# Seven products per expert in a written order over four PSUM rings, the f16 part of h three products later, the squares of the next W1 in the second product

## The chip, the cores and the metric

The kernel runs on one core of a Trainium2 chip. The metric is the device time of one execution in microseconds, as the median of the runs; the run shown by the profile is one execution of its own. Engines are named as in the profile: PE is the matmul engine, PEld its weight loads, DVE the vector engine, ACT the scalar engine, POOL GpSimd, SP the engine whose queue issues the DMAs.

## The reference

Three layers follow each other. Attention over q, k, v (2 x 8 heads x 576 x 64) gives x, 1152 tokens by 512. A mixture of eight experts follows, in which every expert sees every token:

```
P = exp(x @ w_gate - max); 8 times: rows to sum 1, columns to sum N / 8
out = sum over e of P[:, e] * (relu(x @ w1[e]) @ w2[e])      # w1[e]: 512 x 1024, w2[e]: 1024 x 512
```

A last feed-forward layer uses h = out @ w_in, g = h * tanh(softplus(h)), g @ w_out, with w_in and w_out in float64. Inputs and result of the experts are float32.

## The kernel before

**Arithmetic.** A float32 operand is scaled by a power of two and cut into an f16 part (`hi`) and an f16 rest (`lo`); a product is hi·hi + hi·lo + lo·hi, three matmuls per piece of 128 rows. The scale of a weight matrix comes from its sum of squares: four ACT operations (L234, each with an accumulator read behind it), a DVE sum, a POOL all-reduce and some small DVE operations (L64 to L74).

**First product of an expert** (`G1_7`, experts 1 to 7; expert 0 runs another way). x @ w1[e] is done by Winograd's form of Strassen with seven half-size products M1 to M7 instead of eight. There are eight groups (2 token halves of 576 x 4 columns of 128), so 56 products of six matmuls (L966, 288 columns each) in one stage. In a group M1, M6, M5 and M3 accumulate one after the other in one PSUM bank; between them ACT copies the running sum out (L935, a snap: s1, s2, s3). M2 has a bank of its own, M7 and M4 share a third. DVE adds a snap to M2, M7 and M4 (L939), ACT copies M3 out (L980); two halves make a row `r` of 576 tokens. `parts` then lets ACT write the f16 part of relu(r) to h (L947) and DVE, three products later, the rest (L948). A product that accumulates in a bank must wait until the snap of its predecessor has been read.

**Order.** `order7` places the 56 products by due times and by distances (four products from M1 to M6, M6 to M5, M5 to M3). Where nothing fits it leaves a gap, in which `fill` does one of the eight pieces of the second product's first tile (`Head`). Every group takes its three banks from all eight in turn (`mm_tile`).

**Second product** (`G2`): nine tiles of 128 tokens, each 24 matmuls of 512 columns (L995) into one bank, and a DVE operation (L1024) that adds the tile, times P, to acc.

**Work in the background.** Generators in three queues move by one step at each `tick`, in both products. In the first product of expert e: squares and scale of W2[e], its f16 parts (ACT L210, DVE L223), then the load of W1[e+1] and its squares and scale. In the second product: the sums of W1[e+1] that Strassen needs with their f16 parts (`sums_gen`, ACT L266, DVE L269, L273), then the load of W2[e+1]. W1 and W2 share two raw buffers. A third queue (`spare`) converts w_in and w_out from float64 (`Split64`, DVE L343 to L359, L381, L384, L409; ACT L331, L380, L383, L403) over experts 1 to 6. Each engine runs its instructions in the order in which the program issues them, and so does SP with its DMAs.

Of the kernel before, what the change touches and what calls it, by code (L numbers as in the profile page):

```python
# [21 lines left out]
def attn_moe_moe2_kernel(ctx: ExitStack, tc: tile.TileContext, q, k, v, w_gate, w1, w2, w_in, w_out, out):  # L22
# [203 lines left out]
    class SplitSq(Split):  # L226


        def scale_gen(self):
            mx = sm.tile([128, 4], F32, tag="sq", name="sq")  # L230
            for i, r in enumerate(self.raw):
                for c in range(2):
                    junk = late["junk"].tile([128, 1024], BF16, tag="junk", name="junk")
                    nc.scalar.activation(out=junk, in_=r[:, c * 1024:(c + 1) * 1024], func=AF.Square,  # L234
                                         accum_out=mx[:, 2 * i + c:2 * i + c + 1])
                    yield
            m1 = sm.tile([128, 1], F32, tag="m1", name="m1")
            nc.vector.tensor_reduce(out=m1, in_=mx, axis=AX.X, op=ALU.add)  # L238
            ma = all_max(m1)
            for _ in range(3):  # L240
                yield
            self.s, self.inv = scale_from_squares(ma, "sc_" + self.name, self.spare)
            yield

    class SplitSums(SplitSq):
# [56 lines left out]
    class Split64:  # L302
# [94 lines left out]
        def parts_out(self, f, a, b, m):  # L397


            sc = s_out[:, f, :]  # L400
            powers(exponent(m), 266, sc)
            for w in (a, b):
                nc.scalar.activation(out=w, in_=w, func=AF.Copy, scale=sc.bitcast(F32)[:, 0:1])  # L403
            yield
            t = self.w32()
            hw = CW // 2

            def sub(out, u, v):
# [411 lines left out]
    def mm_banks(n):  # L820
        i = len(mm_pools)
        mm_pools.extend([(ps_pool(f"mm{i}", n), f"mm{i}")] * n)
# [71 lines left out]
    SEVEN = dict(M1=(A11_, "B11", "X", None), M6=(S2_, 1, "X", "M1"), M5=(S1_, 0, "X", "M6"), M3=(S4_, "B22", "X", "M5"),  # L894
                 M2=(A12_, "B21", "Y", None), M7=(S3_, 2, "Z", None), M4=(A22_, "T4", "Z", "M7"))

    def order7():


        at = dict(M1=0, M6=4, M2=5, M5=8, M7=9, M3=13, M4=17)  # L900
        todo = sorted((7 * g + t, g, m) for g in range(FT) for m, t in at.items())
        when, order = {}, []
        while todo:
            n = len(order)
            for t, g, m in todo:
                before = SEVEN[m][3]
                if m in "M2 M7" and (g, "M1" if m == "M2" else "M5") not in when:
                    continue
                if t <= todo[0][0] + 14 and (not before or n - when.get((g, before), n) >= (6 if m == "M4" else 4)):
                    when[g, m] = n  # L910
                    order.append((g, m))
                    todo.remove((t, g, m))
                    break
            else:
                order.append(None)
        return order

    def G1_7(w, h, fill):

        open_, lows = {}, []

        def factor(b, n, p, i):
            if n == "T4":
                return xs[b][:, p, i, CH:2 * CH]
            if isinstance(n, str):
                k, j = int(n[1]) - 1, int(n[2]) - 1
                return xs[b][:, p, 2 * k + i, j * CH:(j + 1) * CH]  # L930
            return xt[b][:, p, n, i, :]
# [12 lines left out]

        def parts(n, b, f, r):
            hi, lo = [h[f][:, p, 2 * b * CH:2 * (b + 1) * CH] for p in range(2)]
            nc.scalar.activation(out=hi, in_=r, func=AF.Relu)  # L947
            lows.append((n + 3, lambda: nc.vector.scalar_tensor_tensor(out=lo, in0=r, scalar=0.0, in1=hi, op0=ALU.max,  # L948
                                                                       op1=ALU.subtract)))

        for n, item in enumerate(order7()):
            if item is None:
                fill()
            else:
                gi, m = item
                b, f = gi // 4, gi % 4
                g = open_.setdefault(gi, {})
                a, bn, bank, before = SEVEN[m]
                if not before:
                    g[bank] = mm_tile()[:, 0:CH]  # L960
                ps = g[bank]
                k = 0
                for i in range(2):
                    for wi, xi in ((0, 0), (0, 1), (1, 0)):
                        c = i * 512 + f * 128
                        nc.tensor.matmul(ps, lhsT=w.part(wi, a)[:, c:c + 128], rhs=factor(b, bn, xi, i),  # L966
                                         start=(not before and k == 0), stop=(k == 5), skip_group_check=True)
                        k += 1
                if m == "M1":
                    g["s1"] = snap("s1", ps, 2)  # L970
                elif m == "M6":
                    g["s2"] = snap("s2", ps, 3)
                elif m == "M5":
                    g["s3"] = snap("s3", ps, 2)
                elif m == "M2":
                    add(row(g, "r1")[:, 0:CH], ps, g["s1"])
                elif m == "M7":
                    add(row(g, "r2")[:, CH:2 * CH], ps, g["s3"])
                elif m == "M3":
                    nc.scalar.activation(out=g["r1"][:, CH:2 * CH], in_=ps, func=AF.Copy, scale=HSC)  # L980
                    parts(n, b, f, g["r1"])
                else:
                    add(g["r2"][:, 0:CH], ps, g["s2"])
                    parts(n, b, f + 4, g["r2"])
            while lows and lows[0][0] <= n:
                lows.pop(0)[1]()
            if n % 2 or n % 8 == 0:
                tick(more=n % 6 == 5)
        while lows:
            lows.pop(0)[1]()  # L990

    def G2_products(ps, w, h, t, ft):
        ws = slice(ft * DM, (ft + 1) * DM)
# [4 lines left out]
    class Head:  # L998
# [5 lines left out]
        def __call__(self):  # L1004
            assert self.w.whole and self.n < FT
            if self.ps is None:
                self.ps = mm_tile()
            G2_products(self.ps, self.w, self.h, 0, self.n)
            self.n += 1

    def G2(e, w, h, t, pc, between=None, head=None):
        ps = head.ps if head and head.n else mm_tile()
        for ft in range(FT):
            if not head or ft >= head.n:
                G2_products(ps, w, h, t, ft)
# [90 lines left out]
    with tc.manual_schedule():  # L1106
# [90 lines left out]
        for nm, n in (("junk", 1), ("r", 6), ("wx", 1), ("ws", 1), ("xt", 1), ("sn", 1)):  # L1197
            late[nm] = sb_pool("late_" + nm, n, late_cm)

        early_cm = ExitStack()  # L1200
# [26 lines left out]
        first.drain()  # L1227
        second.drain()
        sp_cm.close()
        mm_banks(2)  # L1230

        def finish(e):
            pc = const.tile([128, NTT], F32, name=f"pc{e}")
# [27 lines left out]
        for e in range(1, E):  # L1261
            h = new_h()
            if e == 1:
                second.add(W2[1].scale_gen(), W2[1].split_gen(), float64_gen(), scale0_gen(), W1[2].scale_gen())
            else:
                second.add(wait_gen(2), W2[e].scale_gen(), W2[e].split_gen())
                if e + 1 < E:
                    second.add(load_gen(W1[e + 1], 8), W1[e + 1].scale_gen())
            head = Head(W2[e], h)
            G1_7(W1[e], h, head)  # L1270
            second.drain()
            pc = finish(e)
            if e + 1 < E:
                second.add(W1[e + 1].sums_gen(), wait_gen(2), load_gen(W2[e + 1], 0))
                for t in range(NTT):
                    G2(e, W2[e], h, t, pc, head=None if t else head)
                second.drain()
# [319 lines left out]
```

## Time and profile before

| | |
|---|---|
| three runs | 1035.18, 1035.9, 1037.35 us; median 1035.9 |
| span of the profiled execution | 1034.6 us, so about 1.3 us of the median lie around the span |
| PE busy | 978.5 us, 95% of the span |
| DVE, ACT, POOL busy | 724.6 us (70%), 510.6 us (49%), 98.0 us (9%) |
| chain that ended last, by engine | PE 73%, DVE 12%, ACT 9%, DMA 2%, issue 2% |
| its costliest lines | L995 34%, L966 15%, L1379 9%, L1446 8%, L939 2%, L948 2%, L210 2%, L234 2% |

The profile was taken in one execution, whose own total time is not listed apart from the span. Busy shares are means over stages with different limits. From 204.56 us (first product of expert 1) to 804.53 us (rest of the second product of expert 7) the program alternates between first and second products, and nearly all of that time PE is busy. A busy PE row overlaps its neighbour: two successive matmuls start closer together than one is shown to last.

### The profile page before, as it was taken

The numbers are of one execution on the slowest core, as the hardware profiler recorded it, in microseconds if no ns is written. First come the engines' busy times: TensorE is split into PE (matmuls) and PEld (weight loads), VectorE is DVE, ScalarE is ACT, GpSimd is POOL, SyncE is SP. The second block draws the span as 40 slices with busy tenths as digits, with TensorE's granted clock in tenths as the row PEclk, the third lists the DMA queues.
The fourth block names the chain that finished last, engine by engine and source line by source line (L and its number), as shares of the span: only waits on it lengthen the run. The fifth ranks groups of instructions, "written<-read, shape, count | busy, mean of one in ns | idle before, by whom it ended". The sixth has DMA issues, their size and how long they took to land.

```text
span 1034.6 us, 17830 instructions
## 1 busy us (share of the span) xinstructions
PE 978.5 (95%) x7185; PEld 656.4 (63%) x7185; DVE 724.6 (70%) x1552; ACT 510.6 (49%) x951; POOL 98.0 (9%) x127
## 2 busy tenths in 40 slices
PE   5889998888999999999999999999999999999998
PEld 4567565466467547645754664575467566988897
DVE  7788649657968796796879669787936456545531
ACT  5667435266357727634672674276346222333431
POOL 6653244000000000000000000000000000000000
PEclk9669998999999999999999999999999999999999
DMA  8962020201243151315314221521300710100010
GB/s 166 211 170 83 17 82 1 81 31 53 84 142 123 50 173 41 123 44 182 122 41 156 70 112 51 183 77 47 133 11 1 316 50 21 68 16 16 6 63 32
DMA packets 83589, 89.25 MB, mean 86 GB/s; under 512 B 34610, under 2 KB 67890, under 8 KB 82226
## 3 DMA queue, kind: packets, MB, share of 16 engines
q1 hardware_dynamic: 83506, 88.11, 27.1%
q8 instruction: 56, 0.92, 0.4%
q14 instruction: 27, 0.22, 0.1%
HBM read 73.15 MB, written 14.94 MB: 85 GB/s over the span
## 4 chain that ended last, share of the span: by engine, by line
PE 73%; DVE 12%; ACT 9%; DMA 2%; issue 2%; POOL 1%; SPq 1%; DVEq 0%; POOLq 0%; ACTq 0%
PE mm L995 34%; PE mm L966 15%; PE mm L1379 9%; PE n L1446 8%; PE mm L845 3%; DVE r L939 2%; DVE h L948 2%; ACT wbh L210 2%; ACT junk L234 2%; ACT h L947 2%; ACT s L935 1%; DMA raw<-in_moe_w_dram 1%; DVE wbl L223 1%; PE at L587 1%; PE at L742 1%
## 5 line engine op out<-in xcount | busy, mean ns | idle before, releaser
L995 PE MATMUL mm<-wbh,h 128*128 128x512 f16 x1152 | 360.0, 382 | 0.0
L995 PEld LDWEIGHTS <-h 128*128 128x128 f16 x1728 | 168.6, 99 | 191.6 <-issue 6.6
L995 PE MATMUL mm<-wbl,h 128*128 128x512 f16 x576 | 220.1, 382 | 0.0
L966 PE MATMUL mm<-x,wah 128*128 128x288 f16 x672 | 129.2, 286 | 0.0
L939 DVE SCALAR_TENSOR_TENSOR r<-mm,s 128x288 f32<-128x288 f32 x168 | 75.2, 454 | 72.1 <-PE mm L966 39.0
L966 PEld LDWEIGHTS <-wx 128*128 128x128 f16 x1008 | 98.6, 98 | 33.8 <-issue 8.4
L966 PEld LDWEIGHTS <-wah 128*128 128x128 f16 x896 | 87.5, 98 | 48.1 <-issue 22.7
L947 ACT ACTIVATE h<-r 128x576 f16<-128x576 f32 x112 | 76.3, 683 | 74.7 <-DVE r L939 72.5
L1379 PE MATMUL mm<-xc,win 128*128 128x256 f16 (+1 forms) x960 | 107.6, 262 | 0.0
L966 PE MATMUL mm<-xt,wx 128*128 128x288 f16 x672 | 100.6, 286 | 3.2 <-ACT s L935 3.2
L966 PE MATMUL mm<-x,wal 128*128 128x288 f16 x336 | 96.1, 286 | 0.0
L1379 PEld LDWEIGHTS <-win 128*128 128x128 f16 x960 | 87.2, 98 | 13.3
L948 DVE SCALAR_TENSOR_TENSOR h<-r,h 128x576 f16<-128x576 f32 x112 | 84.0, 750 | 1.2 <-ACT h L947 1.1
L935 ACT ACTIVATE s<-mm 128x288 f32<-128x288 f32 x168 | 65.3, 399 | 39.2 <-PE mm L966 38.8
L1388 ACT ACTIVATE tt<-mm,cf 128x512 f32<-128x512 f32 (+1 forms) x40 | 25.8, 645 | 113.1 <-PE mm L1379 111.3
L1395 DVE TENSOR_TENSOR tt<-tt 128x128 f32<-128x128 f32 x128 | 31.6, 288 | 68.8 <-ACT tt L1388 67.7
L95 POOL PARTITION_ALL_REDUCE ma<-m x25 | 10.9, 438 | 651.0 <-DVE m L238 397.7
L966 PE MATMUL mm<-xt,wah 128*128 128x288 f16 x224 | 43.4, 285 | 18.6 <-ACT s L935 18.4
L1024 DVE SCALAR_TENSOR_TENSOR acc<-mm,pc,acc 128x512 f32<-128x512 f32 x63 | 46.6, 745 | 14.7 <-PE mm L995 14.5
L234 ACT ACTIVATE junk<-raw 128x1024 bf16<-128x1024 f32 x52 | 54.7, 1051 | 0.2
L966 PE MATMUL mm<-x,wx 128*128 128x288 f16 x336 | 50.3, 286 | 3.1 <-ACT s L935 3.1
L845 PE MATMUL mm<-x,wah 128*128 128x288 f16 x256 | 51.0, 299 | 0.0
(237 smaller groups left out, 1452.4 us busy)
## 6 DMA issues: line engine op xcount, KB each, us to landing
raw<-in_moe_w_dram SPq DMA_DIRECT2D x32, 1024.0 KB, 8.0
f<-in_moe_w_in_dram SPq DMA_DIRECT2D x16, 512.0 KB, 3.9
f<-in_moe_w_out_dram SPq DMA_DIRECT2D x16, 512.0 KB, 3.4
scr<-st SPq DMA_DIRECT2D x32, 256.0 KB, 2.2
scri<-st SPq DMA_DIRECT2D x16, 256.0 KB, 2.6
win<-scri SPq DMA_DIRECT2D x2, 2048.0 KB, 7.8
vw<-in_v_dram SPq DMA_DIRECT2D x30, 96.0 KB, 7.0
qk<-in_k_dram SPq DMA_DIRECT2D x16, 144.0 KB, 3.4
```

Source lines behind the costliest of these rows:

```text
L234: nc.scalar.activation(out=junk, in_=r[:, c * 1024:(c + 1) * 1024], func=AF.Square, accum_out=mx[:, 2 * i + c:2 * i + c + 1])
L845: nc.tensor.matmul(self.ps, lhsT=wt[:, ws], rhs=x[:, xi, kk, o:o + CH], start=(n == 0), stop=(n == 3 * KT - 1))
L935: nc.scalar.activation(out=t, in_=ps, func=AF.Copy, scale=HSC)
L939: nc.vector.scalar_tensor_tensor(out=out, in0=ps, scalar=HSC, in1=r, op0=ALU.mult, op1=ALU.add)
L947: nc.scalar.activation(out=hi, in_=r, func=AF.Relu)
L948: lows.append((n + 3, lambda: nc.vector.scalar_tensor_tensor(out=lo, in0=r, scalar=0.0, in1=hi, op0=ALU.max, op1=ALU.subtract)))
L966: nc.tensor.matmul(ps, lhsT=w.part(wi, a)[:, c:c + 128], rhs=factor(b, bn, xi, i), start=(not before and k == 0), stop=(k == 5), skip_grou ...
L995: nc.tensor.matmul(ps, lhsT=h[ft][:, hi, t * 128:(t + 1) * 128], rhs=wt[:, ws], start=(ft == 0 and n == 0), stop=(ft == FT - 1 and n == 2))
L1024: nc.vector.scalar_tensor_tensor(out=a, in0=ps, scalar=pc[:, t:t + 1], in1=a, op0=ALU.mult, op1=ALU.add)
L1379: nc.tensor.matmul(ps[:, q_ * n:(q_ + 1) * n], lhsT=win[q_][:, wi, f, ws], rhs=x[:, xi, kk, :], start=(m == 0), stop=(m == 3 * KT - 1))
L1395: nc.vector.tensor_tensor(out=a[o], in0=a[u], in1=a[v], op=op)
L1446: nc.tensor.matmul(ps, lhsT=gt(c, f)[:, gi, a, :], rhs=wout[b][:, wi, f, :], start=(k == f == n == 0), stop=(k == len(terms) - 1 and f == ...
```

## The change

The planner `order7` is replaced by a written list of 56 products and two gaps. Four rings of banks replace the turn over all eight: X (M1, M6, M5, M3) has four banks, Z (M7, M4) two, Y (M2) one, H (`Head`) one; the tiles of the second product of experts 1 to 6 have a fixed list of banks. The f16 part of h on ACT comes three products after its row, and the rest on DVE six products after it. The last of a group's first three results to come may now be M2 or M3. The squares and the scale of W1[e+1] move from the end of the first product of expert e to the start of its second product, ahead of `sums_gen`. The written-out dump of the squares uses the buffer of `sums_gen`'s first sum. There is one more step in `scale_gen` and in `parts_out`, and s1 and s2 get a buffer more each.

```diff
-                    junk = late["junk"].tile([128, 1024], BF16, tag="junk", name="junk")
+                    junk = late["ws"].tile([128, 1024], BF16, tag="ws", name="junk")
...
             self.s, self.inv = scale_from_squares(ma, "sc_" + self.name, self.spare)
+            yield
             yield
...
             powers(exponent(m), 266, sc)
+            yield
             for w in (a, b):
...
-    def order7():
...
+    ORDER7 = (
+        "0M1 1M1 0M2 2M1 3M1 0M6 1M6 1M2 2M6 3M6 0M5 0M7 1M5 1M7 2M5 0M3 2M2 1M3 0M4 4M1 1M4 2M3 2M7 3M5 3M7 4M6 "
...
+    RINGS = dict(X=(2, 3, 4, 5), Z=(0, 1), Y=(6,), H=(7,))
+    ring_n = dict.fromkeys(RINGS, 0)
...
+    def ring_tile(name):
+
+        ring = RINGS[name]
+        ring_n[name] += 1
+        return bank_of(ring[(ring_n[name] - 1) % len(ring)])
...
         def parts(n, b, f, r):
             hi, lo = [h[f][:, p, 2 * b * CH:2 * (b + 1) * CH] for p in range(2)]
-            nc.scalar.activation(out=hi, in_=r, func=AF.Relu)
-            lows.append((n + 3, lambda: nc.vector.scalar_tensor_tensor(out=lo, in0=r, scalar=0.0, in1=hi, op0=ALU.max,
+            lows.append((n + 3, lambda: nc.scalar.activation(out=hi, in_=r, func=AF.Relu)))
+            lows.append((n + 6, lambda: nc.vector.scalar_tensor_tensor(out=lo, in0=r, scalar=0.0, in1=hi, op0=ALU.max,
                                                                        op1=ALU.subtract)))
...
                 if not before:
-                    g[bank] = mm_tile()[:, 0:CH]
+                    g[bank] = ring_tile(bank)[:, 0:CH]
...
-                    g["s1"] = snap("s1", ps, 2)
+                    g["s1"] = snap("s1", ps, 3)
                 elif m == "M6":
-                    g["s2"] = snap("s2", ps, 3)
+                    g["s2"] = snap("s2", ps, 4)
...
+    RING2 = (7, 2, 3, 4, 5, 0, 1, 7, 6)
+
     def G2(e, w, h, t, pc, between=None, head=None):
-        ps = head.ps if head and head.n else mm_tile()
+        ps = head.ps if head and head.n else bank_of(RING2[t]) if 0 < e < E - 1 else mm_tile()
...
                 if e + 1 < E:
-                    second.add(load_gen(W1[e + 1], 8), W1[e + 1].scale_gen())
+                    second.add(load_gen(W1[e + 1], 8))
...
-                second.add(W1[e + 1].sums_gen(), wait_gen(2), load_gen(W2[e + 1], 0))
+                second.add(W1[e + 1].scale_gen(), W1[e + 1].sums_gen(), wait_gen(2), load_gen(W2[e + 1], 0))
```

ACT in the middle of expert 2's first product, before. `s1`, `s2`, `s3` are snaps, `mm2_3712` is the bank of the fourth group (3M1, then 3M6), `h_3533<-r_3653` the f16 part of the second group's row that 1M4 completes, `wbh` a quarter of W2's f16 part:

```order
L935 ACTIVATE s1_3719<-mm2_3712 128x288
L210 ACTIVATE wbh_3721<-raw_3326,sc_w2_2_3707 128x1024
L935 ACTIVATE s3_3730<-mm6_3583 128x288
L947 ACTIVATE h_3533<-r_3653 128x576
L210 ACTIVATE wbh_3721<-raw_3326,sc_w2_2_3707 128x1024
L935 ACTIVATE s2_3761<-mm2_3712 128x288
L980 ACTIVATE r_3611<-mm6_3583 128x288
L947 ACTIVATE h_3530<-r_3611 128x576
```

ACT in the same part of expert 2's first product, after. `r_3549`, `r_3599` and `r_3701` are copies of 0M3, 1M3 and 2M3, `s3_3766` is the snap of 3M5, `s1_3731` that of 4M1, and `h_3521<-r_3664` is now the part that 1M4 completes:

```order
L988 ACTIVATE r_3549<-mm2_3524 128x288
L988 ACTIVATE r_3599<-mm2_3533 128x288
L210 ACTIVATE wbh_3710<-raw_3403,sc_w2_2_3689 128x1024
L945 ACTIVATE h_3516<-r_3549 128x576
L933 ACTIVATE s1_3731<-mm2_3724 128x288
L945 ACTIVATE h_3517<-r_3599 128x576
L988 ACTIVATE r_3701<-mm2_3551 128x288
L945 ACTIVATE h_3520<-r_3640 128x576
L210 ACTIVATE wbh_3710<-raw_3403,sc_w2_2_3689 128x1024
L933 ACTIVATE s3_3766<-mm5_3563 128x288
L945 ACTIVATE h_3521<-r_3664 128x576
```

The snap of 3M6 no longer stands behind `h` of 1M4 and a quarter of W2: it was issued ahead of all rows of the second piece, and `h` of 1M4 stands behind the snap of 3M5.

ACT at the end of expert 2's first product, before (`junk,sq` are the squares of W1[3], `st` is a part of Split64):

```order
L935 ACTIVATE s3_4010<-mm2_3930 128x288
L234 ACTIVATE junk_4013,sq_4012<-raw_3884 128x1024
L947 ACTIVATE h_3533<-r_3954 128x576
L234 ACTIVATE junk_4033,sq_4012<-raw_3884 128x1024
L383 ACTIVATE st_4035<-w32_3490,s_in_84 128x512
L935 ACTIVATE s2_4045<-mm6_3995 128x288
L234 ACTIVATE junk_4047,sq_4012<-raw_3886 128x1024
L234 ACTIVATE junk_4058,sq_4012<-raw_3886 128x1024
L980 ACTIVATE r_3984<-mm2_3930 128x288
L947 ACTIVATE h_3530<-r_3984 128x576
L935 ACTIVATE s3_4083<-mm6_3995 128x288
```

The same end, after (from the copy of 7M3 on):

```order
L988 ACTIVATE r_4058<-mm5_3930 128x288
L945 ACTIVATE h_3522<-r_4006 128x576
L945 ACTIVATE h_3519<-r_4058 128x576
L945 ACTIVATE h_3523<-r_4041 128x576
L234 ACTIVATE junk_4108,sq_4107<-raw_3876 128x1024
L384 ACTIVATE st_4110<-w32_3371,s_in_84 128x512
L234 ACTIVATE junk_4120,sq_4107<-raw_3876 128x1024
L384 ACTIVATE st_4122<-w32_3647,s_in_84 128x512
L234 ACTIVATE junk_4132,sq_4107<-raw_3878 128x1024
L234 ACTIVATE junk_4143,sq_4107<-raw_3878 128x1024
```

The four squares stand behind the last snap, copy and f16 part of the stage, where before they stood among them.

DVE in the middle of expert 2's first product, after. `r_3758<-mm0_3751,s2_3609` is the add of 2M4, after which bank `mm0_3751` of ring Z is free for 4M7; `h` are the rests of h, `wbl` those of W2, `w32` is Split64:

```order
L937 SCALAR_TENSOR_TENSOR r_3758<-mm0_3751,s3_3672 128x288
L946 SCALAR_TENSOR_TENSOR h_3517<-r_3599,h_3517 128x576
L223 SCALAR_TENSOR_TENSOR wbl_3711<-raw_3403,sc_w2_2_3689,wbh_3710 128x1024
L349 TENSOR_SCALAR bits_3713<-f64_3257 128x512
L350 SCALAR_TENSOR_TENSOR w32_3647<-w32_3647,bits_3713 128x512
L937 SCALAR_TENSOR_TENSOR r_3780<-mm0_3773,s3_3766 128x288
L946 SCALAR_TENSOR_TENSOR h_3520<-r_3640,h_3520 128x576
L223 SCALAR_TENSOR_TENSOR wbl_3711<-raw_3403,sc_w2_2_3689,wbh_3710 128x1024
L946 SCALAR_TENSOR_TENSOR h_3521<-r_3664,h_3521 128x576
L937 SCALAR_TENSOR_TENSOR r_3811<-mm6_3804,s1_3570 128x288
L946 SCALAR_TENSOR_TENSOR h_3518<-r_3701,h_3518 128x576
L937 SCALAR_TENSOR_TENSOR r_3758<-mm0_3751,s2_3609 128x288
```

Between the adds of 2M7 and 2M4, both in `mm0_3751`, ten other operations now stand in DVE's queue.

## Rows read from the trace of the kernel before

**Rows 1.** Windows, all first and second products of experts 1 to 7; columns ahead

```profile
core 0: us, PE busy (x) PEld busy (x) DVE busy (x) ACT busy (x) POOL busy (x), PEclk, DMA share, GB/s
204.56:804.53 599.97, 575.09 (x3661) 357.88 (x3660) 464.08 (x920) 334.91 (x606) 9.55 (x21) 1.00 0.26 88
```

**Rows 2.** Waits of PE in that stretch: total us, times, longest

```profile
PE mm L966 <- ACT s L935: 24.7, 26, 2.9
```

**Rows 3.** Timeline of PE, expert 1 and expert 2, first products

```profile
212.65 0.90 PE L966 MATMUL mm<-xt,wx 128*128 128x288 f16 x6
213.38 0.90 PE L966 MATMUL mm<-x,wx 128*128 128x288 f16 x6
...
222.08 0.29 PE L966 MATMUL mm<-x,wal 128*128 128x288 f16 x1
223.63 0.41 PE L966 MATMUL mm<-xt,wah 128*128 128x288 f16 x2 [1.26 <-ACT s L935]
...
317.96 0.40 PE L966 MATMUL mm<-xt,wah 128*128 128x288 f16 x2 [1.47 <-ACT s L935]
```

**Rows 4.** Timeline of ACT, middle of expert 2's first product

```profile
315.89 0.68 ACT L947 ACTIVATE h<-r 128x576 f16<-128x576 f32 x1 [1.56 <-DVE r L939]
316.48 1.13 ACT L210 ACTIVATE wbh<-raw,sc_w 128x1024 f16<-128x1024 f32 x1
317.51 0.39 ACT L935 ACTIVATE s<-mm 128x288 f32<-128x288 f32 x1
```

**Rows 5.** Waits of ACT, whole span

```profile
ACT h L947 <- DVE r L939: 72.5, 49, 3.2
```

**Rows 6.** Timeline of ACT, end of expert 2's first product

```profile
340.22 1.04 ACT L234 ACTIVATE junk<-raw 128x1024 bf16<-128x1024 f32 x1
341.39 1.06 ACT L234 ACTIVATE junk<-raw 128x1024 bf16<-128x1024 f32 x1
342.36 0.19 ACT L234 ACTIVATION_READ_ACCUMULATOR junk<-raw 128x1 f32 x1
```

**Rows 7.** Windows, first and second product of expert 2

```profile
298.68:344.64 45.96, 42.42 (x338) 32.84 (x337) 32.71 (x70) 33.88 (x68) 1.05 (x3) 1.00 0.26 92
344.64:390.70 46.06, 46.06 (x219) 21.13 (x217) 42.59 (x82) 17.00 (x23) 0.38 (x1) 1.00 0.38 126
```

**Rows 8.** Timeline of DVE, expert 2's first product

```profile
317.99 0.42 DVE L348 TENSOR_SCALAR bits<-f 128x512 int32<-128x512 int32 x1
318.45 0.69 DVE L349 SCALAR_TENSOR_TENSOR w<-w,bits 128x512 int32<-128x512 int32 x1
319.06 1.28 DVE L223 SCALAR_TENSOR_TENSOR wbl<-raw,sc_w,wbh 128x1024 f16<-128x1024 f32 x1
...
322.00 1.28 DVE L223 SCALAR_TENSOR_TENSOR wbl<-raw,sc_w,wbh 128x1024 f16<-128x1024 f32 x1
323.19 0.45 DVE L939 SCALAR_TENSOR_TENSOR r<-mm,s 128x288 f32<-128x288 f32 x1
323.56 0.75 DVE L948 SCALAR_TENSOR_TENSOR h<-r,h 128x576 f16<-128x576 f32 x1
324.22 0.68 DVE L352 SCALAR_TENSOR_TENSOR w<-f,w 128x512 int32<-128x512 int32 x1
```

**Rows 9.** Timeline of DVE, the last tiles of two second products

```profile
299.06 1.40 DVE L1024 SCALAR_TENSOR_TENSOR acc<-mm,pc,acc 128x512 f32<-128x512 f32 x2
...
386.07 0.17 DVE L74 TENSOR_SCALAR s_in<-ab 128x2 int32<-128x2 int32 x1
...
390.90 0.75 DVE L1024 SCALAR_TENSOR_TENSOR acc<-mm,pc,acc 128x512 f32<-128x512 f32 x1 [0.99 <-PE mm L995]
```

**Rows 10.** SP's issue of W2[3], and DMA issues by line (median us to landing)

```profile
372.81 1.14 SPq L155 DMA_DIRECT2D raw<-in_moe_w_dram  x2
raw<-in_moe_w_dram SPq DMA_DIRECT2D x32, 1024.0 KB, 8.0
```

**Rows 11.** Windows, a stretch of expert 0 behind a wait of PE

```profile
172.11:179.37 7.26, 7.26 (x21) 3.02 (x22) 6.99 (x13) 2.71 (x3) 1.02 (x1) 0.56 0.00 0
```

More of the change, by code (lines that the diff above doesn't have):

```diff
@@ L895, in attn_moe_moe2_kernel, with bank_of @@
                  M2=(A12_, "B21", "Y", None), M7=(S3_, 2, "Z", None), M4=(A22_, "T4", "Z", "M7"))
-    def order7():
[L900 to L916, printed above, removed]
+    ORDER7 = (
+        "0M1 1M1 0M2 2M1 3M1 0M6 1M6 1M2 2M6 3M6 0M5 0M7 1M5 1M7 2M5 0M3 2M2 1M3 0M4 4M1 1M4 2M3 2M7 3M5 3M7 4M6 "
+        "5M1 3M2 3M3 2M4 4M5 3M4 5M6 4M7 4M2 4M3 6M1 5M5 5M7 7M1 4M4 6M6 5M3 5M2 7M6 5M4 6M5 6M7 6M2 7M5 7M7 6M3 "
+        "7M2 - 6M4 7M3 - 7M4")
+    RINGS = dict(X=(2, 3, 4, 5), Z=(0, 1), Y=(6,), H=(7,))
+    ring_n = dict.fromkeys(RINGS, 0)
+    def bank_of(i):
+        pool, tag = mm_pools[i]
+        return pool.tile([128, 512], F32, tag=tag, name=tag)
+    def ring_tile(name):
+        ring = RINGS[name]
+        ring_n[name] += 1
+        return bank_of(ring[(ring_n[name] - 1) % len(ring)])
     def G1_7(w, h, fill):
@@ L946, in parts, with due @@
             hi, lo = [h[f][:, p, 2 * b * CH:2 * (b + 1) * CH] for p in range(2)]
-            nc.scalar.activation(out=hi, in_=r, func=AF.Relu)
-            lows.append((n + 3, lambda: nc.vector.scalar_tensor_tensor(out=lo, in0=r, scalar=0.0, in1=hi, op0=ALU.max,
+            lows.append((n + 3, lambda: nc.scalar.activation(out=hi, in_=r, func=AF.Relu)))
+            lows.append((n + 6, lambda: nc.vector.scalar_tensor_tensor(out=lo, in0=r, scalar=0.0, in1=hi, op0=ALU.max,
                                                                        op1=ALU.subtract)))
-        for n, item in enumerate(order7()):
+        def due(n):
+            lows.sort(key=lambda x: x[0])
+            while lows and lows[0][0] <= n:
+                lows.pop(0)[1]()
+        for n, word in enumerate(ORDER7.split()):
+            item = None if word == "-" else (int(word[0]), word[1:])
             if item is None:
@@ L958, in G1_7 @@
                 a, bn, bank, before = SEVEN[m]
+                g[m] = True
                 if not before:
-                    g[bank] = mm_tile()[:, 0:CH]
+                    g[bank] = ring_tile(bank)[:, 0:CH]
                 ps = g[bank]
@@ L975, in G1_7 @@
                 elif m == "M2":
-                    add(row(g, "r1")[:, 0:CH], ps, g["s1"])
+                    add((g["r1"] if "r1" in g else row(g, "r1"))[:, 0:CH], ps, g["s1"])
+                    if "M3" in g:
+                        parts(n, b, f, g["r1"])
                 elif m == "M7":
@@ L979, in G1_7 @@
                 elif m == "M3":
-                    nc.scalar.activation(out=g["r1"][:, CH:2 * CH], in_=ps, func=AF.Copy, scale=HSC)
-                    parts(n, b, f, g["r1"])
+                    half = (g["r1"] if "r1" in g else row(g, "r1"))[:, CH:2 * CH]
+                    nc.scalar.activation(out=half, in_=ps, func=AF.Copy, scale=HSC)
+                    if "M2" in g:
+                        parts(n, b, f, g["r1"])
                 else:
@@ L984, in G1_7 @@
                     parts(n, b, f + 4, g["r2"])
-            while lows and lows[0][0] <= n:
-                lows.pop(0)[1]()
+            due(n)
             if n % 2 or n % 8 == 0:
                 tick(more=n % 6 == 5)
-        while lows:
-            lows.pop(0)[1]()
+        due(1000)
     def G2_products(ps, w, h, t, ft):
@@ L1006, in __call__ @@
             if self.ps is None:
-                self.ps = mm_tile()
+                self.ps = ring_tile("H")
             G2_products(self.ps, self.w, self.h, 0, self.n)
             self.n += 1
+    RING2 = (7, 2, 3, 4, 5, 0, 1, 7, 6)
     def G2(e, w, h, t, pc, between=None, head=None):
-        ps = head.ps if head and head.n else mm_tile()
+        ps = head.ps if head and head.n else bank_of(RING2[t]) if 0 < e < E - 1 else mm_tile()
         for ft in range(FT):
@@ L1196, in attn_moe_moe2_kernel @@
         late_cm = ExitStack()
-        for nm, n in (("junk", 1), ("r", 6), ("wx", 1), ("ws", 1), ("xt", 1), ("sn", 1)):
+        for nm, n in (("r", 6), ("wx", 1), ("ws", 1), ("xt", 1), ("sn", 1)):
             late[nm] = sb_pool("late_" + nm, n, late_cm)
@@ L1229, in attn_moe_moe2_kernel @@
         sp_cm.close()
-        mm_banks(2)
+        mm_banks(1)
+        mm_banks(1)
         def finish(e):
@@ L1263, in attn_moe_moe2_kernel @@
             if e == 1:
-                second.add(W2[1].scale_gen(), W2[1].split_gen(), float64_gen(), scale0_gen(), W1[2].scale_gen())
+                second.add(W2[1].scale_gen(), W2[1].split_gen(), float64_gen(), scale0_gen())
             else:
```

## The prediction

> **What bounds the kernel now.** I read the page's busy shares first (PE 95%), then the windows, the waits of PE, and the timelines around the longest waits. From 204.56 to 804.53 us PE is busy for 575.09 of 599.97 us at a granted clock of 1.00, that is at 2.4 GHz [rows 1]. The 24.9 us that it idles there are nearly all one wait: a matmul of the first product waits for a snap of ACT, 26 times, 24.7 us in all, 2.9 at the longest [rows 2]. In the waits view PE waits for no other engine in this stretch, so PE's own work is the floor and the change can win only these waits.
>
> The idle time shown understates a wait, since the end of a matmul overlaps the start of the next. A product of six matmuls takes 213.38 - 212.65 = 0.73 us, 0.12 a matmul; across a wait shown as 1.26 us the starts lie 223.63 - 222.08 = 1.55 us apart [rows 3]. The wait cost 1.55 - 0.12 = 1.43, 0.17 more than shown. Over 26 waits that is 4.4 us, and 24.7 + 4.4 = 29.1 us is all that there is to win.
>
> Why are the snaps late? In the same stretch PE waits until 317.96 for the snap of 3M6 [rows 3]. ACT idles 1.56 us for DVE's r, then does the f16 part of h at 315.89, then a quarter of W2 (1.13 us), and the snap only at 317.51 [rows 4]. ACT runs in order, so a snap stands behind a part of h that waits for DVE. Over the span ACT waits so 49 times, 72.5 us [rows 5]. The second cause is at the end of a stage: squares of W1[e+1] are issued among the last snaps; one starts at 340.22, the next at 341.39, so each holds ACT for 1.17 us [rows 6].
>
> **The change part by part.**
>
> *Order of products.* Before, a product could follow its predecessor in a bank after four products, 4 x 0.735 = 2.9 us; in the written list it is five or six, 3.7 to 4.4 us. A snap takes 0.39 us [rows 4]; so ACT may now be late by some 2 to 3 us before PE notices. No matmul is added. The two gaps instead of four move pieces of the same `Head` tile into the second product: cost 0.
>
> *The f16 part of h three products later.* Three products are 2.2 us. The wait of 1.56 us for r falls inside that, and the snaps that were behind it go ahead. ACT's own time stays: in expert 2's first product ACT is busy 33.88 of 45.96 us [rows 7]. Moving four squares away takes 4.7 us from this. The h tiles are read by the second product, which starts after the last; the last parts are issued at the end of the stage, when ACT has no square before them.
>
> *Four rings instead of eight banks.* This is the part that can cost. A bank of ring Z (M7, M4) is taken again two groups later, and its first user may start only when DVE has added the M4 before. The shortest distances in the list are four products (2.9 us), for 2M4 to 4M7 and 3M4 to 5M7 among others. Ten DVE operations stand between the adds of 2M7 and 2M4. I priced DVE's queue by start to start: L223 323.19 - 322.00 = 1.19; an add 323.56 - 323.19 = 0.37; a rest of h 324.22 - 323.56 = 0.66; Split64's operations 318.45 - 317.99 = 0.46 and 319.06 - 318.45 = 0.61 [rows 8]. A bank can be read 0.2 us after its last matmul's place (stage end at 390.70, add at 390.90 [rows 7, 9]), so product number k (from 0) at 0.735 x (k + 1) + 0.2 us into the stage. The add of 2M7 (number 22) ends 17.5 us into it; two quarters of W2's rest (2.4), four rests of h (2.6), two Split64 operations (1.1) and three adds (1.1) lead to 24.7, where PE could start 4M7 (number 33) at 33 x 0.735 = 24.25. That is a wait of 0.45 us, say 0.5. The same count at the other narrow places gives 0 to 0.4, partly covered by the first shift. Bounds: 0, if Split64 and W2 lag elsewhere; and 2.9, the longest wait of before, for a place where the whole distance is lost. I take 0.5 per stage.
>
> *Bank 6 at the boundary.* The ninth tile of the second product now ends in bank 6, and 0M2, third in the next list, takes that bank. In the trace the last two adds to acc run 299.06 to 300.46 while the first product begins at 298.68; 0M2 could begin at 298.68 + 2 x 0.735 = 300.15 and would wait 0.3 us [rows 7, 9]. After expert 2 DVE had 0.99 us to spare before its last add, 390.90 [rows 9]; that add ends at 391.65, ahead of 390.70 + 1.47 = 392.17, so no wait. With DVE fuller I take 0.3 for each of stages 2 to 6; bounds 0 and 1.4, the two adds in a row.
>
> *Squares into the second product.* ACT is busy 17.00 of 46.06 us there [rows 7], so 4 x 1.17 = 4.7 us on ACT are hidden. DVE is the fuller engine: 42.59 of 46.06 us [rows 7]. The sum of squares and the small operations of the scale come to it, eight of 128 by a few values; one such took 0.17 us [rows 9], so 1.2 to 1.4 us, 44 of 46.06, and it fits as long as DVE's chain does not wait for ACT. If it spills, the spill goes into the next first product, where DVE is busy 32.71 of 45.96: cost 0, unless an add of a product stands behind it.
>
> *W2's load.* SP issued W2[3] at 372.81, 28.2 us into the second product, and such a load lands 8.0 us later [rows 7, 10]. With scale and squares ahead of `sums_gen` in the same generator queue it is issued later, by the 4.7 us of squares and a few ticks, up to 7 us by my estimate: landing by 28.2 + 7 + 8.0 = 43 of 46 us. Its first reader is a square some 4 us into the next stage. So 0, with a margin near 7 us.
>
> *The rest* (one step more in two generators, more buffers of s1 and s2, another buffer for the dump of the squares): their instructions stay, and what slips a few ticks later (Split64) is needed only after expert 7: 0, and at most one such operation in front of an add, 1.2 us once.
>
> Sum: stage 1 (no boundary, Split64 just begins) 0.4; stages 2 to 6: 5 x (0.5 + 0.3) = 4.0; stage 7 0.5; together 4.9 us of new waits. Gain 29.1 - 4.9 = 24.2 us. The span 1034.6 becomes 1010.4; about 1.3 us lie between span and median, so 1011.7, put at 1012 us.
>
> **A rule that speaks against this.** From 204.56 on the granted clock stayed 1.00 through all 26 waits [rows 1]. Once, in expert 0, matmuls behind a wait of PE ran from 172.11 to 179.37 at a mean granted clock of 0.56, near the lower level of 1.2 GHz [rows 11]. The Trainium skill, page "TensorE: Matmul & The Clock Gate", section "A second HAM failure mode: psum-queue depth-cycling", says that cycling through PSUM banks with small idles of TensorE between groups of matmuls can make the clock swing between its levels, at a cost in throughput. Four rings with short waits look like that; here the trace disagrees, as the kernel before cycled through eight banks with idles up to 2.9 us at full clock. If it came nonetheless, once in each of seven stages, the price by the row would be 0.44 x 7.26 = 3.2 us each, 22 us: about 1034, no gain.
>
> **The rivals.**
>
> *All waits go and none comes.* For it: my ledger's excess at Z is half a microsecond, within its error. Against: 42.59 of 46.06 us of DVE. 1034.6 - 29.1 + 1.3 = 1007.
>
> *Part comes back.* DVE is late by some 2 us per stage at rings Z or Y, since it also waits for ACT's later f16 part before each rest of h. For it: quarters of W2 of 1.2 us stand between adds. Against: with 32.71 us of work DVE keeps some 9 us free in a first product of 42 us. 7 x 2 = 14: 1007 + 14 = 1021.
>
> *W2 comes late.* If its load lands over 11 us later than I count, the squares and W2's f16 parts block ACT and the snaps behind them, some 3 to 4 us in each of six stages: 1012 + 18 to 24, about 1030 to 1036, no change or little.
>
> *Slower: DVE decides.* Each first product of a bank waits for DVE's add, which stands behind a rest of h that waits for ACT. If the three places (Z, Y, bank 6) cost PE together more than 29.1 / 7 = 4.2 us per stage, the kernel is slower; at 4.5 us it is 1007 + 31.5 = 1038. Against: before, PE never waited for DVE in this stretch.
>
> **How the numbers follow.** Forecast (new waits of 0.2 to 1.7 us per stage, 1008.5 to 1019) 0.66; all waits gone 0.10; part comes back 0.14; W2 late 0.04; clock 0.02; DVE decides, slower, 0.04. A measurement of this kernel can tell about 0.2%, 2 us, from no change. Faster are the first three and a little of the W2 case: 0.91. Same: half of W2 and clock: 0.03. Slower: 0.04 and the rest of these: 0.06. The range begins at 1006, the floor of 1007 less a microsecond for the spread of the runs, and reaches through most of the part that comes back: 1006 to 1022.
>
> **What would show it.** Right: in the waits of PE, the wait of L966's matmuls for ACT's s falls from 24.7 us to below 3; a wait for DVE's r (adds) or for acc appears, 0.3 to 0.8 us at 4M7, 7M2 or 0M2; ACT's wait for r falls well below 72.5; a first product lasts 42 to 43 us instead of 45.96, a second stays at 46.06; squares stand in the second product's window, with ACT near 21.7 there; the clock stays 1.00. Wrong: several waits of over 1 us for DVE in each first product; a second product longer than 46.3; a first square of W2 that waits for its DMA.

## The result and the profile after

The changed kernel takes 1009.68 us (median of four runs, 1008.81 to 1011.54) against 1035.54 before: a ratio of 0.9752, interval 0.9738 to 0.9766. The forecast was 1012. The profiled execution has a span of 1007.1 us.

The two profiles differ in two places. The work before expert 1's first product took 204.56 us before and 201.76 after. Its instructions are the same in both, and in the twelve kernels profiled here it lasted from 200.8 to 206.1, and kernels that differ little from the changed one lie at both ends of it, so I do not count those 2.8 us as the change's. From there to the last matmul of the program it was 826.22 us before and 801.32 after: 24.9 us less, where 24.2 were forecast. The rest of the 2.3 us between forecast and median is no larger than the spread of the first part.

The windows that answer [rows 1, 7], of the changed kernel: from expert 1's first product to the rest of expert 7's second product, then the first and the second product of expert 2 (columns as in [rows 1]).

```profile
201.76:775.53 573.77, 570.58 (x3655) 357.46 (x3654) 460.58 (x918) 331.45 (x606) 10.12 (x21) 1.00 0.28 92
289.54:332.58 43.04, 42.62 (x343) 33.46 (x342) 32.84 (x71) 29.89 (x62) 0.71 (x2) 1.00 0.25 89
332.58:377.91 45.33, 45.33 (x213) 20.54 (x210) 40.03 (x73) 19.28 (x28) 1.09 (x2) 1.00 0.36 116
```

The first product of before in [rows 7] was cut at 344.64, the last two pieces of `Head` and the last product too early. With the true end at 346.67 the kernel before has:

```profile
298.68:346.67 47.99, 44.45 (x350) 34.02 (x349) 34.60 (x77) 34.34 (x69) 1.05 (x3) 1.00 0.25 88
346.67:390.70 44.03, 44.03 (x207) 19.95 (x205) 40.70 (x75) 16.54 (x23) 0.38 (x1) 1.00 0.40 132
```

Two of the four pieces (0.65 us each) have moved from the first into the second product, so 47.99 to 43.04 and 44.03 to 45.33 belong together: 3.65 us less for expert 2. ACT has 4.5 us less to do in the first product and 2.7 more in the second. The clock stays 1.00.

The waits of PE in this stretch, which answer [rows 2], and that of ACT in [rows 5] (total us, times, longest):

```profile
PE mm L971 <- DVE r L937: 2.7, 7, 0.6
PE mm L971 <- ACT s L933: 0.4, 1, 0.4
```

```profile
ACT h L945 <- DVE r L937: 14.7, 18, 2.4
```

The wait for snaps falls from 24.7 to 0.4 us. Even this 0.4 is none of the old kind: it stands at 0M2 of expert 5, which also waits for DVE's add in bank 6 (see the part on bank 6). A new wait is there, for DVE's adds. PE's timeline in expert 2's first product shows it:

```profile
313.06 0.90 PE L971 MATMUL mm<-xt,wx 128*128 128x288 f16 x6
314.39 0.90 PE L971 MATMUL mm<-xt,wx 128*128 128x288 f16 x6 [0.42 <-DVE r L937]
```

The second row is 4M7 (M7 of the fifth group, since groups count from 0), the 34th product, 24.85 us into the stage. Start to start it is 1.33 us behind the product before it, instead of 0.74. DVE's timeline just before, from the add of 2M7 on:

```profile
306.65 0.46 DVE L937 SCALAR_TENSOR_TENSOR r<-mm,s 128x288 f32<-128x288 f32 x1 [0.35 <-PE mm L971]
307.02 0.75 DVE L946 SCALAR_TENSOR_TENSOR h<-r,h 128x576 f16<-128x576 f32 x1
307.69 1.28 DVE L223 SCALAR_TENSOR_TENSOR wbl<-raw,sc_w,wbh 128x1024 f16<-128x1024 f32 x1
...
312.85 0.45 DVE L937 SCALAR_TENSOR_TENSOR r<-mm,s 128x288 f32<-128x288 f32 x1
313.22 0.75 DVE L946 SCALAR_TENSOR_TENSOR h<-r,h 128x576 f16<-128x576 f32 x1
313.88 0.45 DVE L937 SCALAR_TENSOR_TENSOR r<-mm,s 128x288 f32<-128x288 f32 x1
```

DVE does not pause between the two adds in this bank (columns as in [rows 1]; DVE is busy 7.64 of the 7.68 us to the end of the second):

```profile
306.65:314.33 7.68, 7.31 (x60) 5.70 (x59) 7.64 (x13) 7.51 (x14) 0.00 (x0) 1.00 0.00 1
```

The last add, of 2M4, starts at 313.88 and PE at 314.39. Two more answers to rows of before. At the end of the stage ACT finishes the parts of h before the first square, as the order said (compare [rows 6]):

```profile
333.28 0.68 ACT L945 ACTIVATE h<-r 128x576 f16<-128x576 f32 x1 [0.32 <-DVE r L937]
333.87 1.04 ACT L234 ACTIVATE junk<-raw 128x1024 bf16<-128x1024 f32 x1
```

And SP issues W2[3] 363.18 - 332.58 = 30.6 us into the second product (372.81 - 346.67 = 26.1 before, [rows 10]), behind four stores of `Split64`:

```profile
351.32 11.81 SPq L414 DMA_DIRECT2D scr<-st  x4
363.18 1.12 SPq L155 DMA_DIRECT2D raw<-in_moe_w_dram  x2
```

### The profile page after: what moved, and what is told of

It is laid out like the page before. It is cut to its first block, busy times and chain, and to the rows that moved or that the text cites. A ratio compares the mean times of both kernels' runs of the same rounds, so it can differ in the third digit from the quotient of the medians.

```text
span 1007.1 us, 17880 instructions
## 1 busy us (share of the span) xinstructions
PE 970.8 (96%) x7185; PEld 654.3 (65%) x7185; DVE 724.0 (72%) x1552; ACT 507.4 (50%) x951; POOL 98.8 (10%) x127
## 5 line engine op out<-in xcount | busy, mean ns | idle before, releaser
L971 PE MATMUL mm<-x,wah 128*128 128x288 f16 x672 | 128.1, 286 | 0.4 <-ACT s L933 0.4
L971 PE MATMUL mm<-xt,wx 128*128 128x288 f16 x672 | 97.0, 286 | 2.7 <-DVE r L937 2.7
L946 DVE SCALAR_TENSOR_TENSOR h<-r,h 128x576 f16<-128x576 f32 x112 | 81.7, 750 | 0.6 <-ACT h L945 0.6
L971 PEld LDWEIGHTS <-wal 128*128 128x128 f16 x448 | 43.8, 98 | 11.0
L847 PE MATMUL mm<-x,wah 128*128 128x288 f16 x256 | 49.3, 292 | 0.0
```

The source lines that it names most:

```text
L847: nc.tensor.matmul(self.ps, lhsT=wt[:, ws], rhs=x[:, xi, kk, o:o + CH], start=(n == 0), stop=(n == 3 * KT - 1))
L946: lows.append((n + 6, lambda: nc.vector.scalar_tensor_tensor(out=lo, in0=r, scalar=0.0, in1=hi, op0=ALU.max, op1=ALU.subtract)))
```

## The experiments

The spread of the first 200 us is as large as some of the differences sought. So each run is also read by what PE loses afterwards: between expert 1's first product and the end of the second products, the time from one matmul's start to the next, less the usual one (0.1225 us for 288 columns, 0.2158 for 512), summed where the excess is over 0.08. It contains stretches of low clock. For the kernel before this gives 29.3 us, for the changed one 4.7.

| kernel | median us (ratio to before, interval) | PE loses, us |
|---|---|---|
| before | 1035.5 | 29.3 |
| changed | 1009.7 (0.9738 to 0.9766) | 4.7 |
| changed, f16 part at once | 1014.5 (0.9783 to 0.9812) | 8.2 |
| changed, squares back | 1014.9 (0.9788 to 0.9825) | 9.3 |
| the same, banks 6 and 7 exchanged | 1015.3 (0.9787 to 0.9821) | 8.9 |
| the same, W2 loaded later | 1013.4 (0.9757 to 0.9807) | 4.9 |
| written order and rings alone | 1022.6 (0.9856 to 0.9903) | 18.5 |
| f16 part late alone | 1018.5 (0.9819 to 0.9854) | 11.9 |
| squares moved alone | 1031.5 (0.9945 to 0.9973) | 25.1 |
| both parts on ACT, old order and banks | 1007.0 (0.9705 to 0.9737) | 1.2 |
| changed, ring Z of three banks | 1006.0 (0.9701 to 0.9754) | 2.1 |
| the same, banks 6 and 7 exchanged | 1006.4 (0.9708 to 0.9740) | 1.7 |

**The f16 part of h at once again.**

```diff
-            lows.append((n + 3, lambda: nc.scalar.activation(out=hi, in_=r, func=AF.Relu)))
-            lows.append((n + 6, lambda: nc.vector.scalar_tensor_tensor(out=lo, ...
+            nc.scalar.activation(out=hi, in_=r, func=AF.Relu)
+            lows.append((n + 3, lambda: nc.vector.scalar_tensor_tensor(out=lo, ...
```

> The changed kernel with one part undone: ACT's f16 part of h is issued with its row again, DVE's rest three products later. Theory A (the longer distances of five and six products alone give ACT about 3 us of slack, 0.735 x 5 less a snap of 0.4 and 0.2 for reading): the old block in front of a snap, 1.56 us of waiting for DVE's r, 0.68 for h and 1.13 for a quarter of W2, is 3.4 us and exceeds the slack by a few tenths, a few times a stage: 2 to 6 us come back, 1012 to 1016 us, as waits of PE for ACT's s. Rival B (the delay of the f16 part is the main gain, the order is only packing): the waits of 1.63 and 1.0 to 1.2 us in the middle of each stage come back, 7 x 2.6 = 18 us, near 1028 us.

1014.5 us; 3.5 us more are lost than in the changed kernel. That is a balance: some 6 us come anew as waits for snaps, and most of the 3.3 us of the changed kernel's waits at 4M7 go; DVE's rest of h has moved too, which I take for the reason. The waits of PE and of ACT:

```profile
PE mm L971 <- ACT s L933: 4.1, 10, 0.8
PE mm L971 <- DVE r L937: 1.3, 2, 1.1
...
ACT h L945 <- DVE r L937: 50.2, 47, 2.0
```

Theory A held: ACT waits as often for r as before, but with five or six products of distance only 0.3 to 0.95 us reach PE each time.

**Squares back in the first product.**

```diff
-                    second.add(load_gen(W1[e + 1], 8))
+                    second.add(load_gen(W1[e + 1], 8), W1[e + 1].scale_gen())
...
-                second.add(W1[e + 1].scale_gen(), W1[e + 1].sums_gen(), wait_gen(2), load_gen(W2[e + 1], 0))
+                second.add(W1[e + 1].sums_gen(), wait_gen(2), load_gen(W2[e + 1], 0))
```

(and the same for W1[2] in the line of expert 1)

> The changed kernel with one part undone: the squares and the scale of W1[e+1] stand in the first product of expert e again. Theory A: each square holds ACT 1.17 us, less than the slack of about 3 us that the new distances give, so PE sees little of it: 0 to 2 us more, 1010 to 1012 us. Rival B (the end of a stage has no slack in any order): the 0.88 + 0.68 us of the two waits at the end of each of six stages come back, 9 us, near 1019 us.

1014.9 us, outside of what A said, but not where B looked: at the ends of the stages there is no wait at all, so the squares themselves cost nothing there. The 5 us are one event, at 0M2 of expert 3 (bank 6). PE, then DVE, ACT and SP in the stretch ahead of it:

```profile
383.51 0.29 PE L971 MATMUL mm<-x,wal 128*128 128x288 f16 x1
387.39 0.41 PE L971 MATMUL mm<-x,wah 128*128 128x288 f16 x2 [3.59 <-DVE acc L1033]
```

```profile
374.67 0.69 DVE L382 TENSOR_TENSOR st<-w,st 128x512 f16<-128x512 f32 x1 [7.52 <-ACT st L381]
375.27 0.75 DVE L1033 SCALAR_TENSOR_TENSOR acc<-mm,pc,acc 128x512 f32<-128x512 f32 x1
...
385.94 1.40 DVE L1033 SCALAR_TENSOR_TENSOR acc<-mm,pc,acc 128x512 f32<-128x512 f32 x2
```

```profile
374.00 0.63 ACT L381 ACTIVATE st<-w 128x512 f16<-128x512 f32 x1 [7.58 <-DMA scr<-st]
```

```profile
363.53 0.37 SPq L414 DMA_DIRECT2D scr<-st  x1
363.99 1.09 SPq L155 DMA_DIRECT2D raw<-in_moe_w_dram  x2
365.14 10.61 SPq L414 DMA_DIRECT2D scr<-st  x3
```

Read upwards from the last: W2's load (2 MB) is issued between the first store of `Split64` and the other three. `st` has two buffers, so ACT's next write waits for a store that is queued behind the load, 7.58 us. DVE waits for ACT, all that DVE has to do slips, and the adds of the last two tiles come 3.7 us late for bank 6. Windows of the stretch show the rest of the cost: over the 4 us behind the wait the mean granted clock is 0.60.

```profile
383.50:387.39 3.89, 0.30 (x3) 0.10 (x1) 3.74 (x8) 0.42 (x2) 0.38 (x1) 1.00 0.43 135
387.39:391.44 4.05, 4.04 (x21) 2.59 (x20) 1.74 (x3) 1.68 (x4) 0.00 (x0) 0.60 0.13 31
```

**Two tries on that event.** The first gives the ninth tile bank 7 and the eighth bank 6:

```diff
-    RING2 = (7, 2, 3, 4, 5, 0, 1, 7, 6)
+    RING2 = (7, 2, 3, 4, 5, 0, 1, 6, 7)
```

> The run with the squares back in the first product, with banks 6 and 7 exchanged in the last two tiles of the second product (the ninth tile ends in bank 7, the eighth in 6). There PE waited 3.76 us once, for 0M2 of expert 3 in bank 6, behind DVE's add of the ninth tile, and then ran 4 us at a granted clock of 0.60, which cost 1.4 us more. Theory A (this one wait is all that the squares' place costs): 1014.9 - 5.2 = 1009.7 us, and no stretch of low clock behind it. Rival B (DVE is late by 4 us there, and the next thing that needs it waits, 0M2's own add or 1M2): within 2 us of 1014.9.

1015.3 us, and the wait is still 3.2: rival B. The row at 385.94 says why, both last adds stood together behind the same stall. The second leaves the banks and issues the load later:

```diff
-                second.add(W1[e + 1].sums_gen(), wait_gen(2), load_gen(W2[e + 1], 0))
+                second.add(W1[e + 1].sums_gen(), wait_gen(10), load_gen(W2[e + 1], 0))
```

> The run with the squares back in the first product, with W2's load issued eight ticks later in the second product (wait_gen 10 for 2), so that it stands behind the four stores of Split64 in SP's queue in expert 2's second product, as it does in the changed kernel. In the run with the squares back the load (2 MB) was issued between the first of these stores and the others; ACT then waited 7.6 us for a store, DVE 7.5 us for ACT, the last adds to acc came 3.7 us late and PE waited 3.76 us for bank 6. Theory A (the moved squares won only the place of W2's load behind the stores): the wait at 0M2 of expert 3 goes and with it the low clock behind it, 1014.9 - 5.2 = 1009.7 us, with PE losing 4 to 5 us in all in the seven pairs of products. Rival B (without the squares ahead of it Split64 runs earlier and DVE is late at the boundary in any case): the wait stays, 1013 to 1016 us.

In the trace A held: the wait at 0M2 of expert 3 and the low clock are gone, PE loses 4.9 us, as in the changed kernel (4.7). The waits of PE:

```profile
PE mm L971 <- DVE r L937: 2.7, 7, 0.6
PE mm L971 <- ACT s L933: 0.5, 1, 0.5
```

The times alone do not settle it: the median, 1013.4, lies in B's range, the four runs lie between 1008.93 and 1016.26, and in the profiled one the first part took 206.14 us, 4.4 more than in the profile of the changed kernel.

**Both parts on ACT, old order and banks.** `order7`, the turn over all banks and `mm_tile` put back into the changed kernel (its extra steps and buffers stay in):

```diff
-        for n, word in enumerate(ORDER7.split()):
-            item = None if word == "-" else (int(word[0]), word[1:])
+        for n, item in enumerate(order7()):
...
-                    g[bank] = ring_tile(bank)[:, 0:CH]
+                    g[bank] = mm_tile()[:, 0:CH]
```

> The kernel before with the two parts on ACT alone: the f16 part of h three products later and the squares in the second product; the planner's order of products and the turn over eight banks stay. Theory A (ACT's blocks in front of the snaps were the cause, and with them gone a distance of four products, 2.9 us, is enough): most of the 24.7 us comes, 1009 to 1015 us, and with eight banks in turn there are no waits of PE for DVE's r. Rival B (the distance decides: what ACT still has, a copy, parts of h and quarters of W2 in a row, is over 2.3 us): waits of about 1.5 us per stage and more stay, 1020 us or above.

1007.0 us, below the range of A, and below the changed kernel. The waits of PE and the whole stretch:

```profile
PE mm L987 <- ACT s L950: 0.6, 2, 0.3
```

```profile
204.37:775.96 571.59, 570.90 (x3661) 358.11 (x3660) 462.36 (x919) 334.11 (x606) 10.29 (x21) 1.00 0.28 93
```

PE idles 0.7 us in 571.6. So a distance of four products is enough once ACT has no blocks in front of its snaps; the written order and the rings win nothing beside the two other parts and cost 4.7 - 1.2 = 3.5 us, most of it by ring Z's two banks (last part of this section).

**Each part alone.** On the kernel before, first the f16 part late, with the edit shown in the change:

> The kernel before with one part of the change alone: ACT's f16 part of h three products after its row, DVE's rest six after it. The combination of this part with the moved squares, on the old order, measured 1007.0 us. Theory A (two separate causes, a block for each): the waits in the middle of the stages go, the two at the end of six stages, 0.88 + 0.68 us behind squares, stay: 1007 + 9.4, near 1016 us. Rival B (a square alone, 1.17 us, is shorter than the slack of 2.3 us of a distance of four; it hurt only together with a part of h that waits): the waits at the end go too, near 1008 us.

1018.5 us. The long waits of 1.63 us in the middle are gone but for one of 1.09, those at the ends fall from 0.88 + 0.68 to one of 0.33 to 0.43. The time lies beyond A, but not for A's reason: by the waits at the ends it is nearer to B, a square hurts mostly where a part of h that waits stands beside it. What remains is mostly two waits of PE of 2.79 us (expert 1) and 3.57 us (expert 5), with ACT held by `Split64`. The first is not new. The kernel before has it at the same product, 3.02 us, its longest; PE and ACT there:

```profile
234.04 0.90 PE L966 MATMUL mm<-xt,wx 128*128 128x288 f16 x6 [2.85 <-ACT s L935]
```

```profile
233.03 0.66 ACT L331 ACTIVATE w<-f 128x512 f32<-128x512 f32 x1 [3.25 <-DMA f<-in_moe_w_in_dram]
```

ACT waits for the first load of `Split64`, and the snap stands behind. This is neither a part of h nor a square. The second, ACT and DVE at that place:

```profile
592.83 1.33 ACT L403 ACTIVATE w<-w,s_out 128x512 f32<-128x512 f32 x2 [4.82 <-DVE s_out L74]
```

```profile
592.62 0.17 DVE L74 TENSOR_SCALAR s_out<-ab 128x2 int32<-128x2 int32 x1
595.66 0.46 DVE L939 SCALAR_TENSOR_TENSOR r<-mm,s 128x288 f32<-128x288 f32 x1 [2.87 <-ACT s L935]
```

Here ACT waits in order for a scale of `Split64`. The changed kernel issues this operation one step later, and no such wait of PE is in it, though ACT still waits for these scales (`ACT w L405 <- DVE s_out L74`, 4 times, 9.8 us at the longest); the step was not tried by itself.

Then the squares alone, with the edit shown in the change:

> The kernel before with one part of the change alone: squares and scale of W1[e+1] in the second product. Theory A (two separate causes): the two waits at the end of six stages go, 0.88 + 0.68 us each, 9 us, the waits of 1.63 and 1.0 us in the middle stay: near 1026 us. Rival B (the waits at the end come from the parts of h that wait for r): almost nothing is won, 1033 us or more.

1031.5 us, between A and B. The waits at the ends, 9.1 us, are gone, as A said. But in expert 2's first product PE loses 1.20, 1.63 and 2.13 us anew, and SP shows the same order as above, in the second product before it (ACT waits 9.4 us for a store there; no run moved this load):

```profile
285.44 0.38 SPq L412 DMA_DIRECT2D scr<-st  x1
285.87 1.11 SPq L155 DMA_DIRECT2D raw<-in_moe_w_dram  x2
287.08 12.45 SPq L412 DMA_DIRECT2D scr<-st  x3
```

Last, the written order and the rings alone, both edits on ACT undone:

> The changed kernel with both parts on ACT undone: the written order and the four rings alone, f16 part of h at once, squares in the first product. Theory A (the longer distances take up most of ACT's blocks): some 8 us of waits in the first products, as in the run with the f16 part at once, and 0 to 6 us more for a late add at the boundary in one stage: 1014 to 1021 us. Rival B (squares and parts of h add up at the end of a stage beyond any slack): 1025 us or more.

1022.6 us, between A and B. The waits of PE:

```profile
PE mm L971 <- DVE acc L1033: 7.0, 3, 3.5
PE mm L971 <- ACT s L933: 4.0, 10, 0.8
PE mm L971 <- DVE r L937: 1.3, 2, 1.1
```

The waits for snaps are those of the run with the f16 part at once, and to them come three late adds at bank 6 (1.61, 3.68 and 2.21 us), two of them with a low clock behind.

**Ring Z of three banks.**

```diff
-    RINGS = dict(X=(2, 3, 4, 5), Z=(0, 1), Y=(6,), H=(7,))
+    RINGS = dict(X=(2, 3, 4, 5), Z=(0, 1, 7), Y=(6,), H=(7,))
...
         open_, lows = {}, []
+        ring_n["Z"] = 0
```

> The changed kernel with ring Z (M7, M4) on three banks, bank 7 being shared with the head tile, and starting at its first bank in every stage. In the changed kernel PE loses 0.3 to 0.75 us at the start of 4M7 in six of seven stages, 3.3 us in all, waiting for DVE's add of 2M4. Theory A (only the bank holds 4M7): these go and nothing takes their place, 1009.7 - 3.3 = 1006.4 us. Rival B (DVE is simply late there and the next product that needs it waits instead, 7M2 or a product whose snap or row buffer is not free): PE waits as long at another product, within 1 us of 1009.7.

1006.0 us, as A said. PE's waits in the stretch:

```profile
PE mm L972 <- DVE acc L1034: 0.6, 1, 0.6
PE mm L972 <- DVE r L938: 0.4, 1, 0.4
```

At 4M7 nothing waits any more. With banks 6 and 7 exchanged as well:

> The changed kernel with ring Z on three banks (as in the run before, which lost 2.1 us in the seven pairs of products) and banks 6 and 7 exchanged in the last two tiles of the second product, which takes 0M2 off the ninth tile's add (0.77 us at 0M2 of expert 5 there). Theory A (a late single add): 0.8 us less, near 1005.3 us. Rival B (both last adds come late together, as in the run with the exchange and the squares back, where 3.76 fell to 3.20 us only): within half a microsecond of 1006.0.

1006.4 us; the wait at 0M2 of expert 5 goes from 0.77 to 0.40, which the time cannot show. It is B more than A. This version, the one before it and the old order with both parts on ACT all lie between 1006.0 and 1007.0, and these runs do not separate them.

## Why the prediction was right, and where it was not

**What there was to win.** 29.1 us by idle time and 0.17 per wait; counted start to start 29.3. Right, and with it the floor of 1007: the best versions stand at 1006.0 to 1007.0. The forecast named two causes of the late snaps, parts of h and squares; the longest wait, 3.02 us in expert 1, has a third, `Split64`'s first load.

**Ring Z.** Forecast: PE waits 0.5 us per stage at 4M7, since ten operations of DVE end 24.7 us into the stage. Measured in expert 2: the add of 2M4 ends 313.88 + 0.45 - 289.54 = 24.79 us into it, PE loses 0.59. Over the stages it is 0.32 to 0.75 in six of seven, 3.3 us; three banks took it away, so the cause is shown. In stage 1, put at 0.4, there is none. The forecast misread the list in one place: 3M4 to 5M7 are seven products apart, not four. Four apart in ring Z are 0M4 to 2M7 and 1M4 to 3M7 beside 2M4 to 4M7.

**Bank 6.** 0.3 us for five stages, 1.5 in all; measured one wait, 0.61, at expert 5. Its upper bound was too small: 1.4 us, two adds in a row. Where DVE stalls ahead of them it was 3.7 us (squares back), with low clock behind it 5.2. This is the forecast's slower rival at one of its three places. In expert 2's second product the changed kernel escapes it, since W2's load stands behind the stores there. In expert 4's it does not: the load is issued at 543.99, the four stores from 548.38 on, and the one wait measured is the end of the same chain. ACT, then DVE:

```profile
553.81 0.63 ACT L381 ACTIVATE st<-w 128x512 f16<-128x512 f32 x1 [6.14 <-DMA scr<-st]
```

```profile
554.48 1.49 DVE L382 TENSOR_TENSOR st<-w,st 128x512 f16<-128x512 f32 x2 [4.73 <-ACT st L381]
555.89 1.40 DVE L1033 SCALAR_TENSOR_TENSOR acc<-mm,pc,acc 128x512 f32<-128x512 f32 x2
```

So the 0.3 us in each of five stages, from a fuller DVE, did not come; one stall did. I had priced that load's lateness for its own readers, and not what its being early does to the stores behind it.

**New waits together.** 4.9 forecast, 4.7 measured, but partly by luck: ring Z was put at 3.4 and gave 3.3 at 4M7; bank 6 was put at 1.5 and gave 0.6; 0.52 at 2M7 of expert 3 and 0.23 in expert 7, places that the forecast did not name, nearly made up for it.

**Squares.** That they are hidden in the second product is right: PE idles in neither window of it. Two of the numbers, ACT's and DVE's busy time in a second product, stood on the window that was cut too early. By the true one ACT's time there rose from 16.54 to 19.28 us, less than the 4.7 of four squares, and DVE's fell from 40.70 to 40.03 where I had it rise by 1.4; part of `Split64` has gone elsewhere (three of its reductions, L357, in this window, four before). The first product came to 43.04 us, where the forecast named 42 to 43; the second did not stay as it was, it got the two pieces.

**W2's load.** Forecast: issued 4.7 to 7 us later, at no cost. By the true start of the second product W2[3] is issued 30.6 - 26.1 = 4.5 us later, and no square of W2 waits for its load. Right.

**The order of products.** I put it first, as what gives ACT 2 to 3 us of room. It does that (with the f16 part at once some 6 us of waits for snaps come back, where alone on the old order its delay was worth 17), but with both parts on ACT it is not needed. The gain and the cost of the order were never set against each other in the forecast; the sum was right since it went by what remains.

**The extra steps, put at 0.** The runs of one part alone show waits behind `Split64` that the changed kernel lacks. The wait for its first load, about 3 us at one product of expert 1, is in all three kernels without the steps and in none of the nine with them; in the changed kernel ACT still waits 1.66 us for this load, but no product of PE waits behind it. So 0 was too little, by up to 3 us, if the steps did it. No run tried them by themselves; what of this is theirs and what the squares' or the order's is open.

**The clock.** From 201.76 to 775.53 the granted clock was 1.00, as in [rows 1], with nine waits of PE that cost 0.2 to 0.75 us each. The rival taken from the Trainium skill ("TensorE: Matmul & The Clock Gate", "A second HAM failure mode: psum-queue depth-cycling") did not come with waits of this length; this trace does not show what the section describes.

## What to carry to other kernels

A wait of the bottleneck engine on an engine that runs in order is best taken where it arises: move what blocks in front of the awaited instruction, before a longer distance is bought with fewer buffers. Count the queue of the engine that frees a buffer, operation by operation at its pitch: at 4M7 of expert 2 this gave a wait of 0.45 us against 0.59 measured. At bank 6 the count failed, since there that engine itself waited. And when a step moves, look at what it now stands before and behind in the DMA queue, stores with few buffers above all.

## What the runs showed of the hardware

The mean granted clock of the 4 us behind waits of PE of 2.79, 3.20, 3.68, 3.76 and 2.21 us was 0.59 to 0.67, since for most of that time it stood at 0.50, that is at 1.2 GHz. In the case of 3.68 us (written order and rings alone) it stood there before PE went on at 388.31:

```profile
387.70:388.31 0.61, 0.00 (x1) 0.00 (x1) 0.55 (x1) 0.00 (x0) 0.00 (x0) 0.50 0.00 0
```

It stayed at 1.00 behind others of 3.02 us (kernel before, 234.04) and 3.57 us (f16 part late alone, 595.38). The length of the wait alone does not tell which; what else decides is open. Such a fall cost 1.3 to 1.7 us.

The first 200 us, with the same instructions, took from 200.8 to 206.1 us in twelve profiled executions. For a difference of 1 us in a later part, the spans of the parts tell more than the total.
